# Recurrent outputs written with tokens on partitions in batches 2 to 4 of a fused mLSTM and Fourier-mixing kernel

## The chip, the cores and the metric

The kernel runs on one core of one Trainium2 chip. The metric is the device time of one execution in microseconds (us). Three runs of the kernel before gave 405.6, 406.33 and 408.37 us, median 406.33 us. The profile shown here is of one more execution.

## The reference, cut to what matters

A recurrent cell runs over 4 batches of 8 heads, 768 tokens and 40 features a head. Its output is joined to rows of 320 features, mixed by a two-dimensional Fourier transform (real part), normalised and passed through a two-layer perceptron.

```python
for t in range(S):                       # q, k, v: (4, 8, 768, 40)
    m_new = maximum(f[t] + m, i[t])
    C = exp(f[t] + m - m_new) * C + exp(i[t] - m_new) * outer(v[t], k[t])
    n = exp(f[t] + m - m_new) * n + exp(i[t] - m_new) * k[t]
    y[t] = sigmoid(o[t]) * (C @ q[t]) / maximum(abs(n @ q[t]), 1)
x = y as (batch, token, 8 * 40)
u = x + real(fft2(x))                    # over tokens and features
un = (u - mean) / sqrt(var + 1e-6)
out = u + maximum(un @ w1, 0) @ w2       # 320 -> 1280 -> 320
```

## The kernel before, in words

**Order of the work.** Nothing is scheduled by a planner at run time. Each step is put into a dictionary under a slot and a phase (`at(slot, phase, fn, ...)`, L123), and the steps are emitted in the order of (slot, phase). The phases are EVAC 0, FILL 1, MAIN 2 and FILL_PE 3. Each engine then works through its own instructions in that order and waits where it needs another's result. A slot is about one step of the perceptron. The calls of `plan_batch` at L1298 to L1301 place the batches: the recurrent cell of batch 1 starts at slot 0, that of batch 2 at 32, of batch 3 at 50, of batch 4 at 82 (the code counts batches from 0). The perceptron of the first batch has the slots 31 to 62, those of the others 63 to 94, 95 to 126 and 127 to 158, so the cell of one batch runs beside the perceptron of the batch before it.

**Batch 1** uses `plan_mlstm`: chunks of 128 tokens, outputs with features on partitions, turned by TensorE (`mlstm_turn`) before they are finished.

**Batches 2 to 4** use `plan_halves` (L726), which cuts each of the 6 chunks of 128 tokens into two halves of 64, so that TensorE works in four tiles of 64x64. Chunk c begins at slot s = start + 3c. Its steps are: loads at s-5, the gates' exponentials on ScalarE (`mlstm_exp`), the scaled values and queries on GpSimd (`mlstm_scale_v`, `mlstm_scale_q`), scores and state updates on TensorE at s (`halves_scores`, `halves_to_state`), the state kept by GpSimd and VectorE (`halves_decay`, `halves_add`), the mask on GpSimd, the weighing on VectorE at s+1 (`halves_weigh`). At s+3 TensorE makes the outputs `ph`: from the state (`halves_from_state`, L645) and in two turns from the chunk itself (`halves_from_chunk`, L657). A one-element copy on ScalarE (`halves_between`, L668) stands between those two turns. All products of these steps are recorded under L491, the helper `product`.

In the kernel before, the state `C` and the values `v` are the stationary operands and the queries `qg` and weights `W` the moving ones, so `ph` has features on partitions and 128 tokens in the free dimension. At s+4 ScalarE copies it to SBUF (`halves_gather`, `mlstm_heads`, L559 to L579). Some slots later TensorE turns it with four transposes of 128x128 (`halves_turn`, L677 to L681), into the other side of the same two PSUM banks (`side`, L594). A slot after that VectorE finishes it (`mlstm_finish`, L684 to L703): five instructions that divide by the denominator, apply the output gate `so` and write rows of `x`. The gate's tanh is on ScalarE at s+4 (L583), its load at s (L457).

**Reversed chunks.** The Fourier step folds chunk c on chunk 5-c (`mix_fold`, PAIRS) and wants the tokens of one of them in reverse, with the token at the head of the chunk belonging to its neighbour. Before, chunks 2, 4 and 5 (from 0) are reversed, and it is done in the copies of `mlstm_heads`, where tokens are in the free dimension: a copy with a step of -1, and one-column copies for the first token, two of them by GpSimd through `h_first` (L572, L577).

**SyncE** issues all DMAs in the same order of slots; loads, the reads of `M_d` and `G_d` (maxima and decays kept in DRAM, L439 and L451), and the stores (L1156) share its queue.

**Banks and buffers.** PSUM holds one pair of banks for scores and one for outputs. `so` has four buffers, the loaded keys and values four, `W` three, `Gb` and `qg` two.

Of the kernel before, what the change touches and what calls it, by code (L numbers as in the profile page):

```python
# [19 lines left out]
L = 128  # L20
# [20 lines left out]
BACKWARDS = (2, 4, 5)  # L41
PAIRS = ((0, 5), (1, 4), (2, 3))
ORDER = (0, 5, 1, 4, 2, 3)
M_INIT = -1.0e30
# [8 lines left out]
def kernel(  # L53
# [87 lines left out]
    def gates(gp):  # L141
# [44 lines left out]
        for t in hT_bufs + Cd_bufs:  # L186
            nc.gpsimd.memset(t, 0.0)
# [115 lines left out]

        def maxima_out():
            nc.sync.dma_start(out=M_d.rearrange("c i p t -> p c i t"), in_=M[0:BH].rearrange("p c (i t) -> p c i t", i=2))

        def halves_of_chunks(step):
# [8 lines left out]
            elif step == 1:  # L316
# [3 lines left out]
                nc.sync.dma_start(out=G_d[:, H:].rearrange("c p t -> p c t"), in_=g[H:BH])  # L320
# [12 lines left out]
            else:  # L333
                pt, pd = late["p2"]
                nc.vector.tensor_copy(out=colT[:, :, 1, H:], in_=pt[:, :, H:])  # L335
                nc.vector.tensor_copy(out=decB[:, NP:], in_=pd[:, NP:])

        at(12, FILL + 0.7, maxima_out)
        at(1, FILL + 0.2, parts, last)
# [9 lines left out]
        for n, (s, phase) in enumerate(((16, FILL + 0.2), (18, FILL + 0.3), (19, FILL + 0.4), (21, FILL_PE + 0.5),  # L349
                                        (26, FILL + 0.8))):  # L350
            at(s, phase, halves_of_chunks, n)
# [90 lines left out]
    def mlstm_queries(b, c):  # L442
        return slice(LH if b > 0 and c == 0 else 0, L)
# [40 lines left out]
    def mlstm_mask(b, c):  # L484
        for i in range(2):
            W = chunks[b, c].W[i * LH:(i + 1) * LH]
            nc.gpsimd.affine_select(out=W, in_=W, compare_op=OP.is_ge, fill=0.0, base=0, pattern=[[0, H], [1, LH]],  # L487
                                    channel_multiplier=-1)
# [70 lines left out]
    def mlstm_heads(b, c, ph, parts=False):  # L559

        k = chunks[b, c]
        hT, before = k.hT, hT_bufs[(b * NT + c - 1) % 2]
        if b > 0:
            hT, before = (t.rearrange("p (hip m) t -> p hip m t", hip=2) for t in (hT, before))
        every, first, later = (tuple([slice(None)] * (len(ph.shape) - 1) + [t]) for t in
                               (slice(0, L), slice(0, 1), slice(1, L)))
        if c in BACKWARDS:
            nc.scalar.copy(out=hT[later], in_=backwards(ph, L - 1, L - 1))
            if c > TG:
                nc.scalar.copy(out=hT[first], in_=ph[first])  # L570
            else:
                nc.gpsimd.tensor_copy(out=k.hT[:, :, 0:1], in_=h_first)  # L572
        else:
            for r in (slice(hip * 64, hip * 64 + D1) for hip in range(2)) if parts else (slice(0, L),):
                nc.scalar.copy(out=hT[r], in_=ph[r])
            if c == 0:
                nc.gpsimd.tensor_copy(out=h_first, in_=k.hT[:, :, 0:1])  # L577
        if 0 < c < TG:
            nc.scalar.copy(out=before[first], in_=ph[first])  # L579
# [14 lines left out]
    def side(n):  # L594
        return banks["heads"].rearrange("p hip (s m t) -> p s hip m t", s=2, t=L)[:, n]

    TILES = ((0, 0), (1, 1), (0, 1), (1, 0))

    def columns(c, n):

        return LH if c == 0 else n

    def halves_scores(b, c):
# [5 lines left out]
        for p in range(NP):  # L609
            for hip, i in TILES:  # L610
                r, t = slice(hip * 64, hip * 64 + D), slice(i * LH, (i + 1) * LH)
                product(k.ps[t, hip, p, :], k.qk[r, 1, p, t], k.qk[r, 0, p, t], True)

    def halves_to_state(b, c):
        k = chunks[b, c]
        for p in range(NP):
            for i, hip in TILES:
                if 2 * c + i < NS - 1:
                    r, h, n = slice(i * LH, (i + 1) * LH), hip * NP + p, columns(c, D)
                    product(k.pc[hip * 64:hip * 64 + n, i, p, :], k.k[r, h * D:h * D + n], k.vw[r, h, :], True)  # L620
# [11 lines left out]
    def halves_add(b, c, i):  # L632

        k, n = chunks[b, c], 2 * c + i
        if n == 0:
            nc.vector.tensor_copy(out=halves_state(k, 1), in_=k.pc[:, 0])
        elif n < NS - 1:
            nc.vector.tensor_tensor(out=halves_state(k, i + 1), in0=halves_state(k, i + 1), in1=k.pc[:, i], op=OP.add)  # L638
# [6 lines left out]
    def halves_from_state(b, c):  # L645

        k = chunks[b, c]
        k.ph = side(0)
        for m in range(2):
            for i in range(2):  # L650
                for hip, e in TILES:
                    if 2 * c + i > 0:
                        r, t, p = slice(hip * 64, hip * 64 + D), slice(i * LH, (i + 1) * LH), 2 * m + e
                        product(k.ph[e * 64:(e + 1) * 64, hip, m, t], k.C[i][r, p * D1:p * D1 + LH], k.qg[r, p, t],
                                m == 0 and i == (c == 0))

    def halves_from_chunk(b, c, turn):  # L657
# [4 lines left out]
        for m in range(2):  # L662
            for i, e in TILES:
                hip, n = i ^ turn, columns(c, D1)
                r, h = slice(i * LH, (i + 1) * LH), hip * NP + 2 * m + e
                product(k.ph[e * 64:e * 64 + n, hip, m, r], k.v[r, h * D1:h * D1 + n], k.W[r, h, :], False)

    def halves_between(b, c):  # L668

        nc.scalar.copy(out=warm[0:1, 0:1], in_=chunks[b, c].ph[0:1, 1, 1, L - 1:L])  # L670

    def halves_gather(b, c):
        k = chunks[b, c]
        k.hT = hT_bufs[(b * NT + c) % 2]
        mlstm_heads(b, c, k.ph)

    def halves_turn(b, c):  # L677
        k = chunks[b, c]
        px = side(0 if c == NT - 1 else 1)
        for p in range(NP):  # L680
            nc.tensor.transpose(px[:, p // 2, p % 2], k.hT[:, p, :], ident)  # L681
        k.px = px

    def mlstm_finish(b, c):  # L684

        k = chunks.pop((b, c))
        if c == 0:
            xs[b] = x_bufs[b % 2]
        px = k.px.rearrange("p (a pr) t -> p a pr t", a=2) if b == 0 else k.px
        h1 = px.rearrange("p a pr (two e) -> p a (pr two) e", two=2)  # L690
# [11 lines left out]
        x, sc = (t.rearrange("p (a h d) -> p a h d", a=2, d=D) for t in (xs[b][:, c, 0:DM], k.so))  # L702
        nc.vector.tensor_tensor(out=x, in0=h1[:, :, :, 0:D], in1=sc, op=OP.mult)  # L703

# [21 lines left out]
    def plan_halves(b, s0, stride=3):  # L726
        for c in range(NT):
            s = s0 + stride * c
            end = c == NT - 1
# [16 lines left out]
            at(s + 3, MAIN - 0.1 if end else FILL_PE, halves_from_state, b, c)  # L746
            at(s + 3, MAIN - 0.1 if end else FILL_PE, halves_from_chunk, b, c, 0)
            at(s + 3, MAIN if end else FILL_PE + 0.5, halves_between, b, c)
            at(s + 3, FILL_PE + 3, halves_from_chunk, b, c, 1)
            at(s + 4, FILL - 0.6, halves_gather, b, c)  # L750
            at(s + 4, FILL + 0.35, mlstm_tanh, b, c)
            t = s0 + (7, 10, 13, 16, 19, 19)[c]
            at(t, FILL_PE + 0.5, halves_turn, b, c)
            at(t + 1, MAIN + 0.55, mlstm_finish, b, c)
# [545 lines left out]
    plan_batch(2, 50, 83, s_mlp + 2 * MLP_SLOTS)  # L1300
    plan_batch(3, 82, 115, s_mlp + 3 * MLP_SLOTS)  # L1301
# [102 lines left out]
def _layout(q, k, v, o_gate):  # L1404
# [4 lines left out]
    def token_major(t):  # L1409
        return t.reshape(B, H, NT, L, D).transpose(0, 2, 3, 1, 4)  # L1410

    qkT = np.stack([feature_major(q), feature_major(k)], axis=4)
# [3 lines left out]
    o = o_gate.transpose(0, 2, 1, 3).reshape(B, S, DM)[:, _tokens()]  # L1416
# [29 lines left out]
```

## Time and profile before

| what | value |
|---|---|
| the profiled execution's own time | 410.02 us |
| span from the first to the last instruction | 408.3 us |
| granted TensorE clock, mean | 0.991 |
| TensorE matmul busy | 390.9 us |
| VectorE busy | 281.3 us |
| ScalarE busy | 182.1 us |
| GpSimd busy | 129.1 us |
| chain of waits, share that is TensorE | 80% |

Read it so: busy time is the time in which an engine had an instruction in work; the chain of waits is followed backwards from the last instruction, at each step to whatever released it. Busy time of matmuls is modelled with overlap, so the time between the starts of two matmuls tells more of their cost than the duration of one. By slots, the span is cut about so: start and first batch's cell to 64 us; slots 31 to 50 up to 117 us; 51 to 62 up to 175 us; 63 to 82 up to 216 us; 83 to 94 up to 264 us; 95 to 114 up to 304 us; 115 to 126 up to 345 us; the last perceptron to 408 us.

### The profile page before, as it was taken

What the parts mean: (1) busy time and instruction counts of PE and PEld (TensorE: products, weight loads), DVE (VectorE), ACT (ScalarE), POOL (GpSimd) and SP (SyncE); (2) the same over time, 40 slices, a digit from 0 to 9 for tenths busy, and PEclk for the clock granted to TensorE, in tenths of its full rate; (3) what the DMA queues carried; (4) which work ended last, traced back from release to release, by engine and by line L of the source; (5) the groups of instructions that cost most, each with busy time, mean ns of one, the idle gap of its engine ahead of it and who ended that gap; (6) DMA issues with size and microseconds to landing.
All of it is one profiled execution on the core that took longest, in us unless ns stands there. A gap on an engine that the chain in (4) does not pass through costs nothing.

```text
span 408.3 us, 10669 instructions
## 1 busy us (share of the span) xinstructions
PE 390.9 (96%) x4246; PEld 285.3 (70%) x4246; DVE 281.3 (69%) x669; ACT 182.1 (45%) x510; POOL 129.1 (32%) x228
## 2 busy tenths in 40 slices
PE   8999999999979999998999999998999999999996
PEld 6877555556547677765559998855569997556996
DVE  8789986798846539675874579966764786335652
ACT  6987258577640232555464315553450122455000
POOL 5555314477940641240074233440230000020000
PEclk9999999989999999999999999999999999999999
DMA  7989499487643352375001444300000000000000
GB/s 217 289 229 309 114 232 270 157 240 216 166 119 109 113 136 86 99 206 161 0 10 36 139 122 151 108 4 2 0 2 6 28 33 34 0 0 2 32 34 32
DMA packets 23836, 43.29 MB, mean 106 GB/s; under 512 B 5076, under 2 KB 12972, under 8 KB 23660
## 3 DMA queue, kind: packets, MB, share of 16 engines
q1 hardware_dynamic: 23788, 42.63, 35.8%
q8 instruction: 33, 0.54, 0.6%
q14 instruction: 15, 0.12, 0.1%
HBM read 38.49 MB, written 4.12 MB: 104 GB/s over the span
## 4 chain that ended last, share of the span: by engine, by line
PE 80%; DVE 12%; issue 3%; ACT 3%; POOL 1%; POOLq 0%; DVEq 0%; ACTq 0%
PE po L1203 17%; PE pm L1084 16%; PE po L1147 8%; PE pm L1089 5%; PE pm L1022 5%; PE ph L491 4%; PE ps L491 3%; PE pu L901 3%; PE pz L870 2%; PE ph L681 2%; PE put L944 1%; DVE stats L928 1%; PE pm L1013 1%; PE pz L858 1%; PE ph L532 1%
## 5 line engine op out<-in xcount | busy, mean ns | idle before, releaser
L1153 DVE SCALAR_TENSOR_TENSOR x<-po,rstd,x 128x160 f32<-128x160 f32 (+1 forms) x69 | 26.9, 394 | 38.0 <-PE po L1203 35.3
L1093 DVE TENSOR_TENSOR h<-h,pm 128x384 f32<-128x384 f32 x60 | 30.7, 550 | 31.2 <-PE pm L1084 17.2
L1084 PE MATMUL pm<-uT,w_sb 128*128 128x384 f32 x90 | 37.3, 501 | 0.2 <-DVE uT L1072 0.2
L464 ACT ACTIVATE W<-W,colT 128x64 f32<-128x64 f32 x144 | 37.4, 340 | 0.0
L1147 PE MATMUL po<-w_sb,h 128*128 128x320 f32 x120 | 36.1, 451 | 0.0
L629 POOL TENSOR_TENSOR C<-C,decB 128x164 f32<-128x164 f32 x30 | 17.3, 577 | 55.8 <-DVE C L638 45.5
L487 POOL TENSOR_SCALAR_AFFINE_SELECT W<-W 64x512 f32<-64x512 f32 x36 | 28.3, 785 | 17.2 <-ACT W L464 16.1
L1022 PE MATMUL pm<-uT,w_sb 128*128 128x384 f32 x80 | 31.4, 521 | 0.6 <-issue 0.4
L1147 PEld LDWEIGHTS po<-w_sb,h 128*128 128x128 f32 x120 | 23.0, 196 | 10.0 <-issue 1.6
L1203 PE MATMUL po<-T,S 128*128 128x160 f32 x180 | 28.0, 302 | 0.2 <-DVE x L1153 0.2
L474 POOL TENSOR_TENSOR qg<-qk,Gb 128x512 f32<-128x512 f32 (+1 forms) x21 | 27.2, 1297 | 1.1 <-DMA Gb<-G_d 1.1
L1203 PEld LDWEIGHTS po<-T,S 128*128 128x128 f32 x180 | 25.4, 190 | 1.8 <-DVE x L1153 0.5
L1203 PE MATMUL po<-w_sb,h 128*128 128x160 f32 x180 | 26.4, 301 | 0.0
L1203 PEld LDWEIGHTS po<-w_sb,h 128*128 128x128 f32 x180 | 25.1, 190 | 1.2 <-DVE x L1153 0.3
L1089 PE MATMUL pm<-uT,w1t_sb 64*128 64x384 f32 x120 | 25.4, 510 | 0.0
L670 ACT COPY warm<-ph 1x1 f32<-1x1 f32 x18 | 2.6, 147 | 48.6 <-PE ph L491 44.9
L1084 PEld LDWEIGHTS pm<-uT,w_sb 128*128 128x128 f32 x90 | 15.5, 189 | 12.5 <-DVE h L1093 3.6
L1140 ACT ACTIVATE h<-h 128x384 f32<-128x384 f32 x45 | 23.1, 520 | 2.0 <-DVE h L1093 2.0
L968 POOL TENSOR_TENSOR t<-rstd 128x6 f32<-128x6 f32 x12 | 3.1, 256 | 65.3 <-DVE v L962 64.8
L949 ACT COPY uT<-put 128x384 f32<-128x384 f32 x24 | 11.1, 476 | 26.4 <-PE put L944 26.4
L480 POOL TENSOR_TENSOR vw<-kvt,colT 128x328 f32<-128x328 f32 x23 | 18.2, 792 | 13.6 <-DVE colT L335 11.0
L1022 PEld LDWEIGHTS pm<-uT,w_sb 128*128 128x128 f32 x80 | 14.7, 201 | 10.0 <-issue 3.4
(233 smaller groups left out, 879.8 us busy)
## 6 DMA issues: line engine op xcount, KB each, us to landing
kvt<-in_kv SPq DMA_DIRECT2D x24, 336.0 KB
qk<-in_qkT SPq DMA_DIRECT2D x48, 160.0 KB
raw<-in_w SPq DMA_DIRECT2D x10, 640.0 KB
Gb<-G_d SPq DMA_DIRECT2D x36, 128.0 KB
W<-M_d SPq DMA_DIRECT2D x36, 128.0 KB
so<-in_o SPq DMA_DIRECT2D x24, 160.0 KB
out<-x SPq DMA_DIRECT2D x24, 160.0 KB
ds_sb<-in_dft_s SPq DMA_DIRECT2D x1, 1155.0 KB
```

What stands on the lines that cost most here:

```text
L464: nc.scalar.activation(out=k.W[:, h, :], in_=M, func=AF.Exp, scale=-1.0, bias=colT[:, c, 0, b * H + h:b * H + h + 1])
L474: nc.gpsimd.tensor_tensor(out=k.qg[:, :, t], in0=k.qk[:, 0, :, t], in1=k.Gb[:, :, t], op=OP.mult)
L487: nc.gpsimd.affine_select(out=W, in_=W, compare_op=OP.is_ge, fill=0.0, base=0, pattern=[[0, H], [1, LH]], channel_multiplier=-1)
L491: nc.tensor.matmul(out, w, x, start=start, stop=True, skip_group_check=True)
L1022: nc.tensor.matmul(k.pm[i], w1_sb[:, ch, f0:f0 + L], u[2 * ch], start=(ch == 0 and not ahead), stop=(ch == 1 and ahead), skip_group_check= ...
L1084: nc.tensor.matmul(bank, w, u, start=start, stop=True, skip_group_check=True)
L1089: nc.tensor.matmul(bank, block(w1t_sb, i)[rows], mlp_u(gr, 1)[rows], start=False, stop=True, skip_group_check=True)
L1093: nc.vector.tensor_tensor(out=h, in0=h, in1=bank, op=OP.add)
L1140: nc.scalar.activation(out=h, in_=h, func=AF.Relu, scale=-1.0)
L1147: nc.tensor.matmul(k.po, hidden(gr, f)[:, i * L:(i + 1) * L], w2_sb[:, f, :], start=(f == 0), stop=(f == NFF - 1))
L1153: nc.vector.scalar_tensor_tensor(out=u, in0=po, scalar=k.rstd[:, c:c + 1], in1=u, op0=OP.mult, op1=OP.add)
L1203: nc.tensor.matmul(po, a[:, f], w[:, f], start=start and f == 0, stop=f == half - 1, skip_group_check=True)
```

## The change

Operands change sides in batches 2 to 4. The queries `qg` and the weights `W` become stationary and the state and the values moving, so that `ph` comes out with tokens on partitions and 41 columns a head. `halves_gather` and `halves_turn` are gone. `mlstm_finish` reads `ph` itself, at s+4. Which half of a chunk lies on which partitions is swapped for odd heads, on the host for `v`, `k`, on the chip for the gates (`other_halves`, two more copies of `colT`, the reordered read in `halves_add`).

Chunks 0, 1 and 3 are now the reversed ones. Queries, gates and output gates come reversed from the host or from GpSimd copies (`maxima_out`, `halves_of_chunks`), so their outputs are born reversed; but the reversal must also be shifted by one token, which now is one partition. So for those chunks `mlstm_finish` writes its result over `so`, and `halves_rows`, at s+6, moves 127 rows by a DMA from SyncE into `x`, with single rows by further DMAs and one GpSimd copy. Batch 1 takes over the new choice of reversed chunks in its copies.

Slots: the tanh goes from s+4 to s+3; the last chunk's outputs lose their early place and no product stands any more between the two turns of the chunk part; batch 3 starts at slot 53 in place of 50, batch 4 at 83 in place of 82; one step of the gates' preparation goes from slot 21 to 24.

```diff
-BACKWARDS = (2, 4, 5)
+BACKWARDS = (0, 1, 3)
+RUNS = ((0, 2, True), (2, 3, False), (3, 4, True), (4, 6, False))
...
         def maxima_out():
-            nc.sync.dma_start(out=M_d.rearrange("c i p t -> p c i t"), in_=M[0:BH].rearrange("p c (i t) -> p c i t", i=2))
+            m, in_ = (t.rearrange("p (n t) -> p n t", t=LH) for t in (free[0:BH, 0:S], flat(M, slice(0, NT))))
+            for c0, c1, back in RUNS:
+                n = slice(2 * c0, 2 * c1)
+                nc.gpsimd.tensor_copy(out=m[:, n], in_=backwards(in_[:, n], LH - 1, LH) if back else in_[:, n])
+            m = m.rearrange("p (c i) t -> p c i t", i=2)
+            for odd in range(2):
+                for i in range(2):
+                    nc.sync.dma_start(out=M_d[:, i ^ odd, odd:BH:2].rearrange("c p t -> p c t"), in_=m[odd:BH:2, :, i])
...
     def halves_from_state(b, c):
         k = chunks[b, c]
-        k.ph = side(0)
-        for m in range(2):
-            for i in range(2):
-                for hip, e in TILES:
-                    if 2 * c + i > 0:
-                        r, t, p = slice(hip * 64, hip * 64 + D), slice(i * LH, (i + 1) * LH), 2 * m + e
-                        product(k.ph[e * 64:(e + 1) * 64, hip, m, t], k.C[i][r, p * D1:p * D1 + LH], k.qg[r, p, t],
-                                m == 0 and i == (c == 0))
+        k.ph = banks["heads"][:, :, 0:NP * D1].rearrange("p hip (m d) -> p hip m d", d=D1)
+        for p in range(NP):
+            for hip, i in TILES:
+                if 2 * c + i > 0:
+                    r = slice(hip * 64, hip * 64 + D)
+                    t = queries(c, i)
+                    product(k.ph[t, hip, p, :], k.qg[r, p, t], k.C[i][r, p * D1:(p + 1) * D1], p == 0)
...
     def halves_from_chunk(b, c, turn):
         k = chunks[b, c]
         for m in range(2):
-            for i, e in TILES:
-                hip, n = i ^ turn, columns(c, D1)
-                r, h = slice(i * LH, (i + 1) * LH), hip * NP + 2 * m + e
-                product(k.ph[e * 64:e * 64 + n, hip, m, r], k.v[r, h * D1:h * D1 + n], k.W[r, h, :], False)
+            for j, i in TILES:
+                p, hip = 2 * m + (i ^ j), j ^ turn
+                h = hip * NP + p
+                product(k.ph[queries(c, i), hip, p, :], k.W[rows(j), h, :], k.v[rows(j), h * D1:(h + 1) * D1],
+                        2 * c + i == 0 and m == turn == 0)
...
-    def halves_gather(b, c):
-        k = chunks[b, c]
-        k.hT = hT_bufs[(b * NT + c) % 2]
-        mlstm_heads(b, c, k.ph)
-
-    def halves_turn(b, c):
-        k = chunks[b, c]
-        px = side(0 if c == NT - 1 else 1)
-        for p in range(NP):
-            nc.tensor.transpose(px[:, p // 2, p % 2], k.hT[:, p, :], ident)
-        k.px = px
...
+        k.x = k.so if b > 0 and c in BACKWARDS else xs[b][:, c, 0:DM]
+        x, sc = (t.rearrange("p (a h d) -> p a h d", a=2, d=D) for t in (k.x, k.so))
         nc.vector.tensor_tensor(out=x, in0=h1[:, :, :, 0:D], in1=sc, op=OP.mult)
+
+    def halves_rows(b, c):
+        x, y = xs[b][:, :, 0:DM], chunks[b, c].x
+        def move(out, in_):
+            nc.sync.dma_start(out=out, in_=in_)
+        if c == 2:
+            nc.gpsimd.tensor_copy(out=x[0:1, 1], in_=x[0:1, 2])
+            move(x[0:1, 2], chunks[b, 0].x[L - 1:L])
+        elif c in BACKWARDS:
+            move(x[1:L, c], y[0:L - 1])
+            if c > 0:
+                move(x[0:1, c - 1 if c == 1 else c], y[L - 1:L])
...
-            at(s + 3, MAIN - 0.1 if end else FILL_PE, halves_from_state, b, c)
-            at(s + 3, MAIN - 0.1 if end else FILL_PE, halves_from_chunk, b, c, 0)
-            at(s + 3, MAIN if end else FILL_PE + 0.5, halves_between, b, c)
+            at(s + 3, FILL_PE, halves_from_state, b, c)
+            at(s + 3, FILL_PE, halves_from_chunk, b, c, 0)
+            at(s + 3, FILL_PE + 0.5, halves_between, b, c)
             at(s + 3, FILL_PE + 3, halves_from_chunk, b, c, 1)
-            at(s + 4, FILL - 0.6, halves_gather, b, c)
-            at(s + 4, FILL + 0.35, mlstm_tanh, b, c)
-            t = s0 + (7, 10, 13, 16, 19, 19)[c]
-            at(t, FILL_PE + 0.5, halves_turn, b, c)
-            at(t + 1, MAIN + 0.55, mlstm_finish, b, c)
+            at(s + 3, FILL + 0.35, mlstm_tanh, b, c)
+            at(s + 4, FILL + 0.3 if b == 1 else MAIN + 0.55, mlstm_finish, b, c)
+            at(s + 6, FILL - 0.6, halves_rows, b, c)
...
-    plan_batch(2, 50, 83, s_mlp + 2 * MLP_SLOTS)
-    plan_batch(3, 82, 115, s_mlp + 3 * MLP_SLOTS)
+    plan_batch(2, 53, 83, s_mlp + 2 * MLP_SLOTS)
+    plan_batch(3, 83, 115, s_mlp + 3 * MLP_SLOTS)
```

## The prediction, made before the changed kernel ran

> **What bounds the kernel now.** I read the page first, then the chain of waits, the stages by windows, what TensorE waits for, and the lines of the output path.
>
> ```profile
> span 408.3 us, 10669 instructions
> ...
> PE 390.9 (96%) x4246; PEld 285.3 (70%) x4246; DVE 281.3 (69%) x669; ACT 182.1 (45%) x510; POOL 129.1 (32%) x228
> ...
> q1 hardware_dynamic: 23788, 42.63, 35.8%
> ...
> PE 80%; DVE 12%; issue 3%; ACT 3%; POOL 1%; POOLq 0%; DVEq 0%; ACTq 0%
> ```
>
> TensorE bounds it: 96% busy and 80% of the chain. Work taken off TensorE shortens the kernel if nothing takes its place. The windows (window, then TensorE, weight loads, VectorE, ScalarE, GpSimd, clock, share of the DMA engines) show two neighbours to watch in batch 2's cell (64 to 117 us): VectorE, busy 41.39 of 53 us, and the DMA engines, busy 0.73. In 175 to 216 us DMA is at 0.35.
>
> ```profile
> 64.00:117.00 53.00, 50.63 (x860) 30.23 (x858) 41.39 (x80) 35.47 (x105) 36.30 (x53) 0.97 0.73 208
> 117.00:175.00 58.00, 55.91 (x709) 40.38 (x706) 34.27 (x94) 18.43 (x61) 19.49 (x27) 0.97 0.35 102
> 175.00:216.00 41.00, 39.39 (x403) 22.92 (x392) 30.34 (x75) 22.87 (x62) 13.89 (x30) 1.00 0.35 97
> ```
>
> TensorE's own waits: the largest is for L703, the last instruction of `mlstm_finish`.
>
> ```profile
> PE ph L491 <- DVE x L703: 4.3, 6, 1.3
> PE ps L491 <- issue: 2.1, 1, 2.1
> ...
> PE ph L491 <- ACT warm L670: 0.7, 1, 0.7
> ```
>
> One chunk on TensorE in the timeline (start, duration), and below it the first chunk's state update, whose stationary operand has 64 columns where the others have 40:
>
> ```profile
> 159.12 0.69 PE L491 MATMUL ph<-qg,C 40*64 40x64 f32 x32
> 159.64 0.41 PE L491 MATMUL ph<-W,kvt 64*41 64x64 f32 x16
> 159.86 0.65 PE L491 MATMUL ps<-qk 40*64 40x64 f32 x32
> 160.33 0.49 PE L491 MATMUL ps<-vw,kvt 64*40 64x41 f32 x32
> 160.63 0.41 PE L491 MATMUL ph<-W,kvt 64*41 64x64 f32 x16
> 160.98 0.55 PE L944 MATMUL put<-ident,uc 128*128 128x128 f32 x3
> ...
> 62.56 0.63 PE L491 MATMUL ps<-vw,kvt 64*64 64x41 f32 x32
> 63.12 0.59 PE L1022 MATMUL pm<-uT,w_sb 128*128 128x384 f32 x1
> ```
>
> [...] these small products run at the load's pace: with 64 stationary and 41 moving columns, 32 instructions take 63.12 - 62.56 = 0.56 us, of which 0.12 is the change to large matmuls (the same from_chunk group takes 0.35 before a large one, 0.22 before a small), so 0.44; with 40 stationary and the same 41 moving, 160.63 - 160.33 = 0.30. [...]
>
> **The change part by part** (batches 2, 3, 4; 18 chunks).
>
> *Transposes gone.* 72 of L681; four take 0.436 us from start to the next start (their 0.273 us each overlap). 18 x 0.436 = -7.85 us, all in slots where TensorE is the pacer.
>
> *Operands exchanged.* Equal counts. from_state was 64/64 columns, 0.49 to 0.52 us; after it is 64 stationary and 41 moving: 0.44 by the row above. 15 x 0.06 + 3 half-size x 0.06 = -1.1. from_chunk was 41 stationary and 64 moving, 0.22 to 0.23 for 16; after 64 and 41, 0.22: nothing. Bounds: -4 if the moving side counted (pace 0.30), +1 if the loads overlap worse. I take -1.1.
>
> *The wait for L703.* Before, the turned tile shared the output banks, and its finish stood one slot ahead of the next from_state. After, finish is at s+4 and that from_state at s+6, two slots of about 2 us or more. -4.3, between -5.5 and -2.
>
> *Last chunk.* No product separates the two chunk turns. TensorE must wait until the one-element copy has seen the first turn and run: the matmul's 0.41 plus about 0.25 for the copy and its signals, less the 0.22 after which the second would start, about 0.45 and more if ScalarE is late (0.7 in the row above). 3 x 0.6 less three saved changes of size at 0.12: +1.4 (0.5 to 3).
>
> *VectorE and ScalarE.* `mlstm_finish` has the same five instructions on the same sizes. ScalarE loses 18 copies of 0.58 and small ones, which lay beside TensorE: nothing, as ScalarE is at 45%. GpSimd loses four waits for those copies and gains a 1x320 copy a batch: hidden.
>
> *Start.* GpSimd gets nine copies on few partitions (0.2 to 0.4 us each by its small copies); two of them lie ahead of the fold's work, which has about half a us to spare. `M_d` and `G_d` become 4 DMAs each, 0.3 to 0.4 us of issue apiece; `ds_sb`, queued behind the first four, is issued at 32.09 + 1.2 and first read at 43.5. ScalarE gets 0.35 us at the first chunk of batch 1, where it idles 0.82 soon after. VectorE gets two more copies of `colT` (0.3 us in all) between 56 and 60 us, where its conversions lead the chain. +0.6 (0 to 2).
>
> *The moves.* Nine of 127 rows, 1280 B each, 162.6 KB on one engine. By the page an engine moves 42.63 MB / (0.358 x 16 x 408.3 us) = 18.2 KB/us, so 8.9 us; the trace's 1280 B packets took 55 ns in the median, so 7.0. The folds read the rows five slots after the finish (10 us at 41 us / 20 slots), after a move of 7 to 9 and some 2 us of issue and signals: barely covered, up to 1 us of VectorE twice. Worse is the queue behind. Each move is followed by the load of `so` for the chunk two later, whose tanh now comes at s+3 on ScalarE, just ahead of the one-element copy for which TensorE waits. Before:
>
> ```profile
> 77.80 0.36 SPq L369 DMA_DIRECT2D raw<-in_w  x1
> 78.21 0.42 SPq L457 DMA_DIRECT2D so<-in_o  x1
> ...
> 86.50 0.58 SPq L457 DMA_DIRECT2D so<-in_o  x1
> ...
> 93.67 0.48 ACT L583 ACTIVATE so<-so 128x320 f32<-128x320 f32 x1
> 101.03 0.47 ACT L583 ACTIVATE so<-so 128x320 f32<-128x320 f32 x1
> ```
>
> From issue to use are 15 us, after the change less a slot of 2.65, so 12. The loads landed 4.5 to 6 us after issue; one move brings that to 12 or 14, two within 8 us, with 0.73 of load besides, to more. In batch 2 I count 2.5 us for a late `so`, 1 to 2 for a late `raw` piece (issued at 84.65, its first conversion at 93.23, landed at 90.2 by its packets) and the rest for smaller ones: 4.5. In batches 3 and 4 only the fifth chunk's `so` (from 0) is in fast slots: 0.7 each. +6.0 (0 to 16).
>
> *Later start of batches 3 and 4.* Their waits end with slots to spare; VectorE gets about 3 us more in 175 to 216 us, where it is at 30.34 of 41: nothing, or +1.
>
> Sum: -7.85 - 1.1 - 4.3 + 1.4 + 0.6 + 6.0 = -5.25 on the span of 408.3, which makes 403.05. That execution took 410.02 us, the median is 406.33; taken off the median: **401.1 us**.
>
> **The rivals.**
> 1. *The moves are hidden.* For it: batches 3 and 4 run at a DMA share of 0.35 and slots of 4 to 5 us where most moves lie. Without the 6.0: 395.1. If the small products gain by the moving side too, 392.
> 2. *The one engine becomes the pacer* (slower). Three moves in batch 2 are 21 to 27 us on an engine with 0.73 x 53 = 39 us of its own: 60 to 66 in 53. A late `so` holds ScalarE, and so TensorE, once for each of the nine moves. The gain without moves is 11.25, so 1.25 us of lateness for each decides; at 2.0 it is 18 - 11.25 = +6.75, 413. Against it: only batch 2 is short of DMA time.
> 3. *The gain is given back elsewhere:* VectorE in batch 2, at 41.39 of 53, is late with the weighing behind a held conversion, and waits move to L643. Half of the 12.15 saved by transposes and L703 lost on top of the rest gives about 407, no change.
>
> **How the numbers follow.** Chances: forecast 0.45 (398 to 405), rival 1 0.22 (392 to 398), rival 2 0.18 (over 410.4), rival 3 0.15 (403 to 410). About 1% is what a measurement of this kernel can tell from no change: 402.3 and 410.4. Of the forecast, 0.32 lies under 402.3 and 0.13 above. Faster 0.32 + 0.22 = 0.54; same 0.13 + 0.15 = 0.28; slower 0.18. The range 394 to 410 leaves about 0.2 outside, mostly above; the forecast's own is 398 to 405.
>
> **What would show it.** No L681; from_state at about 0.44 us a chunk; no wait of TensorE for the finish; three waits for the one-element copy of 0.4 to 1 us; ScalarE idle before tanh, or VectorE before the first conversion, released by a DMA in 75 to 115 us, is the moves' price. It is wrong if those waits are absent, or if the fold waits for a DMA for several us.

## The result and the profile after

After the change the kernel takes 417.82 us (median of 4 runs, 415.59 to 420.32), beside 405.97 us for the kernel before on the same chip: a ratio of 1.0287, 95% interval 1.0211 to 1.0363. It is slower by nearly 3% where the forecast had it 1.3% faster. The profiled execution took 420.32 us, its span is 418.6 us. Line numbers below are those of each kernel's own profile; after the change `product` is L519, the one-element copy L699, `mlstm_finish` L712 to L720, the moves L728, the tanh L605, the residual of the perceptron L1183.

The page of after, the same lines as those shown of before:

```profile
span 418.6 us, 10543 instructions
...
PE 390.6 (93%) x4174; PEld 283.7 (68%) x4174; DVE 277.4 (66%) x671; ACT 171.9 (41%) x481; POOL 132.1 (32%) x234
...
q1 hardware_dynamic: 25312, 44.11, 37.0%
...
PE 27%; DVE 2%; issue 1%; ACT 0%; DVEq 0%
```

TensorE has 72 matmuls less and yet the same busy time, 390.6 us beside 390.9: some of them run at half clock. The clock in the trace is 0.5 in five stretches of 3.4 to 6.8 us, 24 us in all ((1 - 0.971) x 418.6 x 2), where before (0.991) had 7.7; large matmuls there start 0.64 us apart and at full clock 0.32. The chain of waits breaks off early here (its shares add up to 30%), so the stages and the engines' own waits have to tell the story. The same three windows as before (window, length, TensorE, weight loads, VectorE, ScalarE, GpSimd, clock, DMA share, GB/s):

```profile
64.00:117.00 53.00, 43.28 (x653) 25.37 (x655) 36.44 (x74) 29.21 (x85) 29.61 (x40) 0.90 0.59 167
117.00:175.00 58.00, 57.69 (x733) 41.03 (x729) 36.48 (x99) 17.69 (x58) 21.21 (x32) 1.00 0.44 122
175.00:216.00 41.00, 36.91 (x453) 21.38 (x444) 24.96 (x67) 16.76 (x48) 12.26 (x24) 0.88 0.52 136
```

In the first TensorE is busy 43.28 us where it was 50.63, at a clock of 0.90 in place of 0.97. The DMA engines are less busy than before (0.59, was 0.73): they are not full on average, though one of the 16, as the packets below show, is the narrow place for a while. The third window, batch 3's cell, loses as well, and there the forecast saw next to nothing. TensorE's own waits (engine, line, what it waited for: us, times, longest):

```profile
PE ph L519 <- ACT warm L699: 10.3, 6, 6.9
PE po L1233 <- DVE x L1183: 2.9, 2, 2.6
PE pm L1119 <- ACT h L1155: 2.5, 2, 1.4
PE ph L519 <- DVE W L672: 1.3, 1, 1.3
```

The wait for L703 (4.3 us before) is gone, and 10.3 us for the one-element copy stand in its place. What holds that copy is seen in ScalarE's waits:

```profile
ACT so L605 <- DMA so<-in_o: 17.1, 6, 6.6
```

The tanh is late for want of `so`. What is behind that is seen in the waits of SyncE's queue:

```profile
SPq L478 <- DMA x<-so: 18.7, 4, 5.6
SPq L728 <- DVE so L720: 16.1, 4, 6.1
...
SPq L396 <- DMA x<-so: 4.8, 1, 4.8
SPq L1186 <- DMA x<-so: 4.7, 2, 4.5
SPq L466 <- DMA x<-so: 4.1, 1, 4.1
```

`x<-so` are the moves. SyncE itself stands still for 32.3 us until moves have landed (18.7 + 4.8 + 4.7 + 4.1), and before the change it had no such wait. The worst place of batch 2 in the timeline (start, duration; the last bracket is the wait):

```profile
80.17 0.70 SPq L728 DMA_DIRECT2D x<-so  x1
80.92 3.25 SPq L484 DMA_DIRECT2D so<-in_o  x1
...
86.93 0.54 SPq L396 DMA_DIRECT2D raw<-in_w  x1
92.75 1.08 SPq L478 DMA_DIRECT2D Gb<-G_d  x2
93.94 4.65 SPq L728 DMA_DIRECT2D x<-so  x2
98.64 0.99 SPq L484 DMA_DIRECT2D so<-in_o  x1
...
107.32 0.47 ACT L605 ACTIVATE so<-so 128x320 f32<-128x320 f32 x1 [6.60 <-DMA so<-in_o]
107.70 0.13 ACT L699 COPY warm<-ph 1x1 f32<-1x1 f32 x1
107.88 0.67 PE L519 MATMUL ph<-kvt,W 64*64 64x41 f32 x16 [6.85 <-ACT warm L699]
```

Count the DMAs that SyncE issues after the first move: `so`, two of `qk`, `kvt`, two of `W`, `raw`, and then the first `Gb`, the eighth. It doesn't go out before 92.75. The trace has eight completion signals for SyncE's DMAs (numbers 101 and 104 to 110), and 206 of 224 DMAs have the same one as the eighth before; none of the 224 goes out before the DMA that had its signal last has landed. This `Gb` has the signal of the move, which lands at 92.69: the slow move has stopped the queue. The packets of 1280 bytes, the move's 127 rows and the 128 of the `so` behind it, show how slow:

```
packets of 1280 bytes begun in each us, from 83 us on
after          83:12 84:39 85:119 86:20 87:11 88:10 89:12 90:12 91:11 92:9 93:0
moves in two   83:199 84:56 85:0
```

In after the 127 rows go one behind the other (0.0517 us a row at 83.4 us) and trickle until 92.6, 9 us for a move that was priced at 7 to 9; from issue to landing it takes 12.5 us (80.17 to 92.69), 3.2 of them ahead of the first row, where the forecast had some 2 for issue and signals. So far the size was foreseen. (Before has no transfer of 127 rows: that the move would run on one engine, and later loads wait behind it there, was the author's assumption, which this trace bears out.) What follows was not: the next move goes out at 93.94, a single row behind it takes 3.93 us to issue, and the `so` goes out at 98.64, where the load stood at 86.5 before. And then it lands late too. The trace has the time at which each of the 16 DMA engines finished its part of a transfer: 15 parts of this `so` are there by 101.53, the last, behind the move's rows, at 107.30. Its tanh, ready at 100.72, runs 6.6 us late, the one-element copy stands behind the tanh, and TensorE waits 6.85 us. Then large matmuls run at half clock: 0.73 granted in 100 to 110 us.

All six waits in the 17.1 us are of this kind. The tanh starts 0.02 us after the last part of its `so`, and the other 15 parts had landed 4.6 to 7.0 us before that one. Had the last part come with the others, 0.8 of the 17.1 us would be left (an estimate from these times).

### The profile page after: what moved, and what is told of

It reads as the page before. It is cut to its first block, busy times and chain, and to the rows that moved or that the text cites. A ratio compares the mean times of both kernels' runs of the same rounds, so it can differ in the third digit from the quotient of the medians.

```text
span 418.6 us, 10543 instructions
## 1 busy us (share of the span) xinstructions
PE 390.6 (93%) x4174; PEld 283.7 (68%) x4174; DVE 277.4 (66%) x671; ACT 171.9 (41%) x481; POOL 132.1 (32%) x234
## 5 line engine op out<-in xcount | busy, mean ns | idle before, releaser
L1183 DVE SCALAR_TENSOR_TENSOR x<-po,rstd,x 128x160 f32<-128x160 f32 (+1 forms) x69 | 27.1, 395 | 45.2 <-PE po L1233 38.6
L652 POOL TENSOR_TENSOR C<-C,decB 128x164 f32<-128x164 f32 x30 | 17.1, 570 | 86.4 <-DVE C L667 74.5
L1114 PE MATMUL pm<-uT,w_sb 128*128 128x384 f32 x90 | 38.8, 521 | 1.7 <-DVE h L1123 1.3
L1177 PE MATMUL po<-w_sb,h 128*128 128x320 f32 x120 | 34.2, 435 | 0.0
L1052 PE MATMUL pm<-uT,w_sb 128*128 128x384 f32 x80 | 31.3, 532 | 0.1
L515 POOL TENSOR_SCALAR_AFFINE_SELECT W<-W 64x512 f32<-64x512 f32 x36 | 26.2, 728 | 12.4 <-ACT W L491 11.1
L501 POOL TENSOR_TENSOR qg<-qk,Gb 128x512 f32<-128x512 f32 (+1 forms) x21 | 28.4, 1354 | 2.4 <-DMA Gb<-G_d 2.4
L519 PE MATMUL ph<-kvt,W 64*64 64x41 f32 x576 | 16.8, 237 | 11.6 <-ACT warm L699 10.3
L1114 PEld LDWEIGHTS pm<-uT,w_sb 128*128 128x128 f32 x90 | 16.0, 195 | 16.2 <-DVE h L1123 7.4
L979 ACT COPY uT<-put 128x384 f32<-128x384 f32 x24 | 11.1, 477 | 30.3 <-PE put L974 30.3
L1052 PEld LDWEIGHTS pm<-uT,w_sb 128*128 128x128 f32 x80 | 15.5, 207 | 11.0 <-issue 3.2
```

The source lines that it names most:

```text
L501: nc.gpsimd.tensor_tensor(out=k.qg[:, :, t], in0=k.qk[:, 0, :, t], in1=k.Gb[:, :, t], op=OP.mult)
L1052: nc.tensor.matmul(k.pm[i], w1_sb[:, ch, f0:f0 + L], u[2 * ch], start=(ch == 0 and not ahead), stop=(ch == 1 and ahead), skip_group_check= ...
L1114: nc.tensor.matmul(bank, w, u, start=start, stop=True, skip_group_check=True)
L1177: nc.tensor.matmul(k.po, hidden(gr, f)[:, i * L:(i + 1) * L], w2_sb[:, f, :], start=(f == 0), stop=(f == NFF - 1))
L1183: nc.vector.scalar_tensor_tensor(out=u, in0=po, scalar=k.rstd[:, c:c + 1], in1=u, op0=OP.mult, op1=OP.add)
```

## The experiments

"First" and "second reading" are the outcomes that an expectation names, in its order. Each experiment is an edit of the kernel after or, where the text says so, of the kernel before or of "two parts", the first experiment; ratios are to the kernel before. A difference is worked out from two ratios times 407 us, about what the kernel before took beside them; where the kernel after is one of the two, it has an uncertainty of some 3 us, nearly all from the four runs of after.

**Moves in two parts.** In after the completion times show 16 parts for each load of `so` with its 128 rows, and one engine for each move of 127 rows. In this run they show 16 engines for the 112 rows.

```diff
-            move(x[1:L, c], y[0:L - 1])
+            move(x[1:113, c], y[0:112])
+            move(x[113:L, c], y[112:L - 1])
```

> Each move of 127 rows is issued as 112 rows and then 15 rows, from the same queue. Theory A (the move runs row by row on one DMA engine, 127 x 0.0517 = 6.6 us, and everything behind it on that engine and behind SyncE's waits is late): the rows spread over many engines, a move lands in under 3 us, ScalarE's waits for so before tanh fall from 17.1 us to under 3, time 394 to 400 us. Theory B (the moves' place and number, the finish they wait for, the tanh a slot earlier, the lost cover): nothing is taken away and nine more DMAs are issued, time 415 to 421.

403.94 us, 0.9935 (0.9913 to 0.9957), clock 0.987. The same rows, nine DMAs more, and 14.3 us less than after ((1.0287 - 0.9935) x 407; 11 to 17.5 by the two intervals). ScalarE has no wait for `so` left, SyncE none for a move, and the packets of a move are over in 2 us. From issue to landing a move takes 2.3 to 5.5 us in place of 9.2 to 12.9, and the `so` behind it 2.4 to 4.3 in place of 8.3 to 12.1. TensorE's waits:

```profile
PE po L1234 <- DVE x L1184: 2.9, 2, 2.6
PE ph L519 <- ACT warm L699: 2.7, 5, 1.1
PE ph L519 <- DVE W L672: 1.3, 1, 1.3
```

Theory A holds in its cause, but its number doesn't: 394 to 400 was expected. With the moves' price nearly gone the gain is (1 - 0.9935) x 407 = 2.65 us, not 11.

**No moves at all.**

```diff
-        k.x = k.so if b > 0 and c in BACKWARDS else xs[b][:, c, 0:DM]
+        k.x = xs[b][:, c, 0:DM]
...
-            at(s + 6, FILL - 0.6, halves_rows, b, c)
```

> The moves and their single rows are left out and the finish writes x itself, so the reversed chunks of batches 2 to 4 are one token off. Theory A: the time is that of the forecast without its moves, 395 us (392 to 399), and the moves cost about 22 us. Theory B: the loss stays, 410 us or more. The forecast's other terms are read from this run's trace: TensorE should wait for the finish for less than 0.5 us, and for the one-element copy for about 2 us in three waits.

407.05 us, 1.0003 (0.9975 to 1.0030): both theories miss. That is slower than with two parts, and the trace has the reason: the finish now writes `x` itself at s+4 and waits for a store of the batch that still owns the buffer, and TensorE waits for the residual behind it. VectorE's wait:

```profile
DVE x L720 <- DMA out<-x: 3.3, 1, 3.3
```

and TensorE's, 5.9 for the residual where two parts have 2.9:

```profile
PE po L1232 <- DVE x L1182: 5.9, 3, 3.0
PE ph L519 <- ACT warm L699: 2.7, 5, 1.1
```

Without those 3.3 us it would be about where two parts are (an estimate; no run has neither the moves nor this wait). By it two parts cost next to nothing, and the missing gain has to be looked for outside the moves.

**Two engines.** 122 rows and 5 in place of 112 and 15.

```diff
-            move(x[1:113, c], y[0:112])
-            move(x[113:L, c], y[112:L - 1])
+            move(x[1:123, c], y[0:122])
+            move(x[123:L, c], y[122:L - 1])
```

> The moves in two parts of 122 and 5 rows in place of 112 and 15. [...] a move takes them about 3.3 us in place of 6.6 on one (estimate: 61 rows x 0.0517 us, the row's time in the trace of the kernel after). If the loss follows the engine's time: half of the 14 us remains, 409 to 413. If only the last few us of lateness reach TensorE (a threshold): 403.5 to 407. If the count of engines is not what matters: 415 to 419.

403.77 us, 0.9920 (0.9890 to 0.9950), as with 16: the reading with the threshold. The completion times show two engines for 122 rows. In the waits of SyncE's queue it still stands for moves, but 13 us in place of 32 and never above 3.6; the tanh waits 1.4 in place of 17.1:

```profile
SPq L466 <- DMA x<-so: 7.5, 3, 3.6
SPq L1187 <- DMA x<-so: 3.0, 1, 3.0
SPq L396 <- DMA x<-so: 2.5, 1, 2.5
```

The loss behaves like a threshold, not like a share: with half of the rows on an engine all of the 14 us are gone. The times fit that: a `so` behind such a move lands 4.6 to 7.7 us after its issue (8.3 to 12.1 in after), and only what exceeds the lead of its issue over its use can reach TensorE.

**Two parts in batch 2 alone.**

```diff
+            for r0, r1 in ((0, 112), (112, L - 1)) if b == 1 else ((0, L - 1),):
+                move(x[r0 + 1:r1 + 1, c], y[r0:r1])
```

> The moves in two parts of 112 and 15 rows in batch 2 alone; batches 3 and 4 keep one DMA of 127 rows. By the forecast's split batch 2 has three quarters of the moves' cost: 407 or less (404 to 408). By the traces of after and of the two parts, in which after falls behind by 7.4 us in batch 2's cell and by 9 more in those of batches 3 and 4, more than half remains: 410 to 413.

410.86 us, 1.0102 (1.0075 to 1.0129), the second reading. Batches 3 and 4 keep (1.0102 - 0.9935) x 407 = 6.8 us of the loss, batch 2 has (1.0287 - 1.0102) x 407 = 7.5. The same large matmuls in the traces of after and of two parts tell much the same: after falls back by 7.4 us up to 112 us, by 7.0 more up to 208, by 2.1 more up to 293 (times of after).

**`so` loaded three slots earlier**, the moves as in after.

```diff
-            at(s, FILL, mlstm_load_o, b, c)
+            at(s - 3, FILL, mlstm_load_o, b, c)
```

> The load of so is issued three slots earlier (s-3 in place of s), the moves unchanged. If the loss comes to TensorE only by the late so and the tanh in front of the one-element copy: ScalarE's 17.1 us of waits for so go, TensorE's 10.3 us at L519 for the copy fall under 3, time 405 to 409 us. If the late loads of qk, W and raw and the fold's rows cost the same again on other engines: 411 to 417.

420.73 us, 1.0349 (1.0285 to 1.0413), if anything slower; both readings miss. The lateness only changes its place, by TensorE's waits and one of ScalarE's:

```profile
PE ph L519 <- DVE W L672: 10.4, 3, 8.4
PE ph L519 <- ACT warm L699: 6.9, 7, 3.5
...
ACT W L491 <- DMA W<-M_d: 15.1, 4, 10.9
```

TensorE now waits 10.4 us for the weighing (1.3 before this edit), and ScalarE 15.1 us for the loads of `W`. So it isn't one load that matters; another load behind a move is late in its place.

**Tanh behind the one-element copy**, the moves as in after.

```diff
-            at(s + 3, FILL + 0.35, mlstm_tanh, b, c)
+            at(s + 3, FILL_PE + 0.6, mlstm_tanh, b, c)
```

> The kernel after with one change: the tanh stands behind the one-element copy on ScalarE, so that a late so no longer holds the copy that TensorE waits for. If the late so costs by that copy: TensorE's 10.3 us of waits for it fall to about 2.5 and the time to 408 to 412 us. If other late loads and the finish hold TensorE instead: 415 to 419.

410.66 us, 1.0080 (1.0052 to 1.0109), as the first theory had it. TensorE's wait for the copy falls from 10.3 to 2.6 us, and the time by (1.0287 - 1.0080) x 407 = 8.4. The tanh a slot earlier, in front of the copy, is thus the path by which 8.4 of the 14.3 us reached TensorE. Its waits:

```profile
PE po L1233 <- DVE x L1183: 3.0, 2, 2.7
PE ph L519 <- DVE W L672: 3.0, 2, 1.5
PE ph L519 <- ACT warm L699: 2.6, 6, 0.7
```

The same edit on two parts, where no `so` is late:

> The kernel with the moves in two parts, and the tanh is put behind the one-element copy on ScalarE (same slot). TensorE waited 1.56 and 1.29 us for that copy near 81 and 83 us, and large matmuls ran at half clock for some 4 us after it, 0.32 us lost on each of seven. If the tanh holds the copy: both waits fall under 0.9 us and 2 to 3 us come back, 401 to 402. If ScalarE is held there by other work: no change, 403.4 to 404.4.

403.46 us, 0.9916 (0.9886 to 0.9947): the second reading, no difference that shows. TensorE's waits near 81 and 83 us are 1.41 and 0.73 us with it, 1.34 and 1.09 without (the expectation counts from start to start, which is some 0.2 us more). The first of them is for the weighing, not for the copy, and VectorE's conversions hold the weighing there.

**Other queues for the moves**, the shape as in after. GpSimd's:

```diff
-            nc.sync.dma_start(out=out, in_=in_)
+            nc.gpsimd.dma_start(out=out, in_=in_)
```

> The moves, unchanged in shape, are issued by GpSimd instead of SyncE. If what costs is that SyncE waits with a later DMA until the move has landed (34 us of such waits in the trace of the kernel after): SyncE goes on, time 398 to 405 us. If what costs is the row after row on one engine, in front of the loads' share on that engine: tanh still waits for so, time 411 to 418. [...]

406.07 us, 0.9974 (0.9947 to 1.0002), between the two readings. It can't tell the two causes apart: on this queue the move was over in about 1 us (32 packets of up to 5120 bytes, not 127 of 1280), so both the slow move and SyncE's waits were gone. ScalarE's:

```diff
-            nc.sync.dma_start(out=out, in_=in_)
+            nc.scalar.dma_start(out=out, in_=in_)
```

> The moves keep their shape (127 rows, row after row on one DMA engine) but are issued by ScalarE, so that no later DMA of SyncE waits until a move has landed. If SyncE's waits (32 us of them for the moves in the trace of the kernel after) are what makes the loads late: 403 to 408 us, ScalarE paying some 0.6 us of issue for each of 18. If the busy engine itself makes the loads late: 413 us or more, with tanh still waiting for so.

429.97 us, 1.0553 (1.0474 to 1.0632). That lies in the second reading's 413 or more, but the sign it named is missing: ScalarE's view has no wait of tanh for `so`. (An issue took ScalarE 0.52 to 1.21 us in 76 to 112 us, where the expectation had some 0.6.) SyncE's waits for moves did fall, from 32.3 to 18.2 us, but ScalarE works through its queue in order as well: it idled 9.50 us until a single row could go out behind a move, and the copy that TensorE needs stood behind that. TensorE's wait for it:

```profile
PE ph L519 <- ACT warm L699: 20.6, 8, 8.1
```

How much of the 14.3 us is SyncE's stop and how much the loads' own parts on the busy engine stays open; no run took one away without the other. For the six waits of the tanh the times in after say more. The busy engine's part came last in all six. SyncE's stop shows in how long before the tanh was ready a `so` went out: for the worst one 2.1 us, where two parts have 11.1; for the other five 5.7 to 11.2 us, where two parts have 3.1 to 11.7. By these times the stop is what made the worst wait so long, together with the engine; four of the other five had about the lead that they have in two parts.

**Where the rest of the gain went.** First the price of the transposes, in the kernel before:

```diff
-        for p in range(NP):
+        for p in (0, 1, 2, 3, 0, 1, 2, 3):
             nc.tensor.transpose(px[:, p // 2, p % 2], k.hT[:, p, :], ident)
```

> The kernel before with its 72 transposes of batches 2 to 4 issued twice (the same tiles into the same places), nothing else. The forecast prices them at 0.436 us for four, 7.85 us in all, all on TensorE's path: 6.5 to 9 us slower than before, 413 to 416 beside a before of 407. If TensorE has slack in those slots (it waits there for VectorE or ScalarE anyway, so that four transposes fill a wait): less than 4 us slower.

413.18 us, 1.0167 (1.0111 to 1.0224), so 6.8 us for 72 (4.5 to 9.1). The 7.85 of the forecast is in it. Then the starts of batches 3 and 4, on two parts:

```diff
-    plan_batch(2, 53, 83, s_mlp + 2 * MLP_SLOTS)
-    plan_batch(3, 83, 115, s_mlp + 3 * MLP_SLOTS)
+    plan_batch(2, 50, 83, s_mlp + 2 * MLP_SLOTS)
+    plan_batch(3, 82, 115, s_mlp + 3 * MLP_SLOTS)
```

> The kernel with the moves in two parts, and batches 3 and 4 start at slots 50 and 82 again. Theory C (the later starts put a finish of batch 4 and its weighing ahead of a residual in slot 87, where TensorE waited 2.8 us and then ran large matmuls at half clock for a few us): 399 to 402 us against 403.9 for the two parts, and the wait of TensorE for the residual falls under 0.5 us. Theory D (it is the finish at s+4 itself that collides, whatever the start): another wait takes its place, 402.5 to 406.

401.03 us, 0.9869 (0.9805 to 0.9933). (With batch 3 at 50 a finish overwrites rows of batch 1 before their residual is added.) With batch 4 alone at 82:

```diff
-    plan_batch(3, 83, 115, s_mlp + 3 * MLP_SLOTS)
+    plan_batch(3, 82, 115, s_mlp + 3 * MLP_SLOTS)
```

> The moves in two parts, and batch 4 alone starts at slot 82 again (batch 3 stays at 53). With both starts back it was 401.0 against 403.9. If the gain is the residual of slot 87 that stood behind a finish and a weighing (2.8 us and the half clock after it): 400.5 to 402. If it came from batch 3: 403.5 to 404.5.

401.78 us, 0.9868 (0.9784 to 0.9951), the fastest complete version, about 2.7 us under two parts, though the intervals overlap. The wait didn't vanish as theory C of the run before had it; it was split. The windows of two parts around it (clock third from the end), and the wait itself in the timeline:

```profile
230.00:240.00 10.00, 7.36 (x42) 6.95 (x41) 7.86 (x28) 0.97 (x2) 2.95 (x4) 0.86 0.21 57
240.00:250.00 10.00, 10.00 (x184) 8.80 (x184) 9.13 (x24) 3.56 (x11) 2.24 (x4) 0.97 0.58 170
...
235.91 1.90 PE L1234 MATMUL po<-T,S 128*128 128x160 f32 x10 [2.64 <-DVE x L1184]
```

and those of the start at 82:

```profile
240.00:250.00 10.00, 8.61 (x174) 7.38 (x173) 9.41 (x20) 3.44 (x10) 4.58 (x6) 1.00 0.21 59
250.00:260.00 10.00, 8.47 (x176) 7.78 (x174) 7.19 (x23) 4.77 (x15) 4.38 (x7) 1.00 0.67 182
...
244.05 1.90 PE L1234 MATMUL po<-w_sb,h 128*128 128x160 f32 x12 [1.39 <-DVE x L1184]
256.46 1.63 PE L1234 MATMUL po<-T,h 128*128 128x160 f32 x10 [1.41 <-DVE x L1184]
```

One stall of 2.64 us from 233 us on, with the clock at 0.86 and 0.97 in these windows, stands against two of 1.39 and 1.41 at full clock. The finish behind the weighing, on two parts:

```diff
-            at(s + 4, FILL + 0.3 if b == 1 else MAIN + 0.55, mlstm_finish, b, c)
+            at(s + 4, MAIN + 0.75, mlstm_finish, b, c)
```

> The moves in two parts, and the finish is put behind the weighing of the same slot on VectorE (and so behind the residual of that slot) in all three batches. If the finish ahead of other work on VectorE is where the forecast gain went (TensorE's waits near 81, 182 and 233 us, for the weighing, the copy and a residual): these fall by half or more, 399 to 402. If the next chunk's state part then waits for the late finish, or if VectorE is simply full there: 403 to 407.

407.05 us, 1.0009 (0.9984 to 1.0035), at the upper end of the second reading, which holds: the wait for the finish, which the change had removed, is back among TensorE's waits.

```profile
PE po L1234 <- DVE x L1184: 3.1, 3, 2.7
PE ph L519 <- DVE x L720: 2.2, 2, 1.3
PE ph L519 <- DVE so L720: 2.0, 1, 2.0
```

At last the cover between the last chunk's two turns, put back on two parts:

```diff
-            at(s + 3, FILL_PE, halves_from_state, b, c)
-            at(s + 3, FILL_PE, halves_from_chunk, b, c, 0)
-            at(s + 3, FILL_PE + 0.5, halves_between, b, c)
+            end = c == NT - 1
+            at(s + 3, MAIN - 0.1 if end else FILL_PE, halves_from_state, b, c)
+            at(s + 3, MAIN - 0.1 if end else FILL_PE, halves_from_chunk, b, c, 0)
+            at(s + 3, MAIN if end else FILL_PE + 0.5, halves_between, b, c)
```

> The kernel with the moves in two parts, and the last chunk's state part, first turn and one-element copy come ahead of the slot's large matmuls again, as in before. The forecast prices the missing cover at 1.4 us in all (three waits of 0.53 us in the trace): 402 to 403 against 403.9. If the wait is covered by nothing that counts, or if the first turn now waits for the weighing instead: 403.5 to 405.

404.16 us, 0.9928 (0.9904 to 0.9952): the second reading, no gain that shows. The three waits for the copy (0.31 us each in the view, 0.5 from start to start) are gone, but an early state part now waits 1.0 us for the finish, 0.4 without the edit. And the edits of two parts, of the start at 82, of the cover and of the tanh together:

> Moves in two parts, batch 4 from slot 82, the last chunk's cover back and the tanh behind the one-element copy, all together. If the small repairs add to the start at 82 (401.8): 399.5 to 401.2. If they were nothing alone because other waits end later: 401.2 to 402.5.

402.89 us, 0.9912 (0.9877 to 0.9946): just above both readings, and not faster than the start at 82 alone.

## Why the prediction was wrong

The sum was -5.25 us, measured are (1.0287 - 1) x 407 = +11.7. Of the 16.9 us between the two, 8.3 are the moves and 8.6 the other terms together.

The first step that failed is the size of the moves' term, "+6.0 (0 to 16)", with its split of 4.5 in batch 2 and 0.7 each in batches 3 and 4. Measured it is 14.3 us, 8.3 more, 7.5 in batch 2 and 6.8 in the other two. The mechanism was named (one engine, later loads behind the move on it, a late `so`, the tanh ahead of the copy), and the time of one move was about right, 9 us. Two things in the term were wrong. It counted with a lead of 12 us, read early in batch 2, and saw one late `so` each in batches 3 and 4, at 0.7 us. Of the six `so` that came late, five had gone out only 2.1 to 7.3 us before their tanh was ready, while a `so` behind a move took 8.3 to 12.1 us to land; in batches 3 and 4 alone the tanh waited 2.64, 1.53 and 2.68 us. And it left out the queue: SyncE doesn't only have loads behind the move on that engine, it stops at the eighth DMA after it, 32.3 us in all, and so the next load, move and load are late together. The `so` behind the second move cost 6.85 us in one piece where 2.5 was written for all of batch 2. That batches 3 and 4 run at a DMA share of 0.35 was no cover, since the mean over 16 engines says nothing of the one that has the move. It is the second rival's case, at 14.3 / 9 = 1.6 us a move.

The second step that failed is that the gain without the moves, 11.25 us, was taken as kept; 2.65 us of it arrived, because VectorE and ScalarE made TensorE wait elsewhere.

Point by point, the other terms:

- *Transposes, -7.85:* right (6.8 by doubling them).
- *Operands, -1.1:* wrong, about nothing. The state part takes 0.487 us (median from start to next start) where 0.44 was estimated; the row it was taken from is another product with other neighbours. Scores with the new order of tiles take 0.494 us, before 0.467. The bound of +1 held it. That the stationary columns set the pace did hold: with 64 of them 32 instructions take about the same with 41 moving columns (0.487 us) and with 64 (0.494). In before four weight loads and their four matmuls start every 0.058 us with 64 stationary and 41 moving columns (62.65 to 62.94 us), and every 0.038 with 40 and the same 41 (160.41 to 160.52). The timeline of two parts (start, duration):

```profile
152.47 0.68 PE L519 MATMUL ph<-C,qg 40*64 40x41 f32 x32
152.96 0.42 PE L519 MATMUL ph<-kvt,W 64*64 64x41 f32 x16
153.19 0.68 PE L519 MATMUL ps<-qk 40*64 40x64 f32 x32
153.69 0.51 PE L519 MATMUL ps<-vw,kvt 64*40 64x41 f32 x32
```

- *The wait for L703, -4.3:* gone, as said, but not kept. `mlstm_finish` costs VectorE the same 1.6 us; that it has "the same five instructions" was right and beside the point. It moved ahead of weighings, residuals and perceptron copies, and TensorE waits for those in two parts: 2.64 us from 233 us on, 1.04 at 267, and in 80 to 90 us, where VectorE is busy 9.79 of 10 us, TensorE takes 2.3 us more than before, half clock included. (0.66 us at 182 are a wait for the copy behind the tanh; with the tanh behind it 0.30.) Put the finish later, and the wait for it comes back (1.0009). This is the third rival's mechanism, beside the second's.
- *Last chunk, +1.4:* right in size (three waits, 0.5 us each from start to start), though its repair brought nothing.
- *Start, +0.6:* right; the large matmuls stand 0.75 us later at 78 us.
- *Later starts, nothing or +1:* probably too low; 2.7 us between start 83 and 82 of batch 4, with overlapping intervals, by the stall at 233 us.
- *Clock:* no term at all. Some stalls are followed by half-speed matmuls: seven of 0.64 us in place of 0.32 at 86 us in two parts. In after it counts for more: some 24 us at half clock beside (1 - 0.987) x 402.2 x 2 = 10.5 in two parts. If half of that time is lost, the difference is some 7 of the moves' 14.3 us (an estimate).

Together the terms without moves brought 2.65 us (0.9935) where 11.25 were counted. TensorE's waits for other engines, apart from those that both have, show where the rest went: 9.3 us in two parts (residual 2.9, one-element copy 2.7, weighing 1.3, the perceptron's hidden values 1.6 and inputs 0.4, finish 0.4), where before had 6.1 (finish 4.3, one-element copy 0.7, weighing 0.5, three of 0.2). So -6.8 for the transposes, +3.2 for the waits and +0.75 for the start make -2.85, about what was measured; it is an estimate that leaves the clock out.

The execution of before that was profiled is not a typical one. It was 3.7 us above the median (410.02 and 406.33) and holds a stall of TensorE of 2.09 us up to 119.17 us ("issue", while 16 KB of instructions were being fetched, 116.6 to 117.7) with half clock after it. That the fetch caused it was not tried. The forecast took its sum off the median, so this is no part of its error. The promised marks were there, all but the state part's 0.44 us: no L681, the waits for the copy, ScalarE before tanh released by a DMA. They showed a price and not its size.

## What to carry to other kernels

Before a DMA is put into a busy queue, find out from a trace how many engines its shape reaches (from SyncE 128 and 112 rows reached 16 here, 122 two and 127 one), and then follow both the engine and the issuing queue: what is loaded behind this DMA, how long before its use each of those loads goes out, and which later DMA waits for this one's completion. Take the lead at the place where it is shortest. A wait that is taken away by moving work earlier on another engine counts as gained only when the places it moved past have been checked for someone waiting there. Moves that reached more than one engine (112 + 15 rows, even 122 + 5, in place of 127) turned 3% slower into 0.65% faster here.

## What the runs showed of the hardware that was not expected

- Two DMA engines for 122 rows were as good as 16 for 112: 403.77 and 403.94 us.
- A DMA of 127 rows from GpSimd's queue went out as 32 packets of up to 5120 bytes and was over in about 1 us, where the same from SyncE went out as 127 of 1280 and took 9. At the 18.2 KB/us of one engine in before, its 162.6 KB in 1 us are the work of some nine engines (an estimate).
- In two parts the clock fell to half for some 3.4 us after a single stall of 2.64 us (windows of 10 us at 0.86 and 0.97: (0.14 + 0.03) x 2 x 10); with batch 4 at 82 it stayed full after stalls of 1.39 and 1.41 us 12 us apart. The length of a stall alone doesn't decide it: near 83 us half clock followed waits of 1.34 and 1.09 us in two parts (0.68 granted in 80 to 90 us), but waits of only 0.54 and 0.75 us in before (0.83). The timeline of before there, the last line with six matmuls in 3.55 us:

```profile
80.63 0.44 PE L491 MATMUL ph<-W,kvt 64*41 64x64 f32 x16 [0.54 <-DVE W L643]
...
82.62 0.43 PE L491 MATMUL ph<-W,kvt 64*41 64x64 f32 x16 [0.75 <-ACT warm L670]
...
83.61 3.55 PE L1022 MATMUL pm<-uT,w_sb 128*128 128x384 f32 x6
```
